# Attention features and a two-layer feed-forward: weights converted from one load by a rounded copy and a difference, with a new order of the first units

## The chip, the core and the metric

The kernel runs on one core of a Trainium2 chip. The metric is device time in microseconds, the median of three runs. The core's engines each work through their own queue in the order in which the program was written: TensorE (PE; its weight loads are PEld), VectorE (DVE), ScalarE (ACT), GpSimd (POOL) and SyncE (SP), which here issues nearly all DMAs.

## The reference

Eight batches of eight heads with 576 positions of 64 dimensions go through an attention with random features (128 features, each used with both signs), and the result, 4608 tokens of 512, through two matrix products with x·tanh(softplus(x)) between them.

```python
def phi(x):
    proj = np.einsum('bhsd,df->bhsf', x, w_phi)
    proj = proj - np.max(np.abs(proj), axis=-1, keepdims=True)
    return np.concatenate([np.exp(proj), np.exp(-proj)], axis=-1)
q_p, k_p = (phi(q), phi(k))
kv = np.einsum('bhsf,bhsd->bhfd', k_p, v)
z = np.sum(k_p, axis=2)
num = np.einsum('bhsf,bhfd->bhsd', q_p, kv)
den = np.einsum('bhsf,bhf->bhs', q_p, z)[..., None] + 1e-06
out = num / den
...
h = x @ w_in                     # 512 -> 2048
g = h * np.tanh(log1p(exp(h)))   # h itself where h > 20
return (g @ w_out).astype(np.float32)
```

w_in and w_out come as 64-bit floats; q, k, v and w_phi as 32-bit floats.

## The kernel before

**Work units.** Keys come in 36 units of 512 rows ("k0" to "k35"), queries in 18 chunks of 256 tokens with two halves each ("q0_0", "q0_1", "q1_0", ...), the values v in 32 tiles. A key unit is loaded, projected on TensorE (`project`, into two tiles pp), its absolute maximum is taken and subtracted on VectorE (`centre`: two reductions, two subtractions), ScalarE takes both exponentials (`exp`), and TensorE adds the products with v (`sum`, into kvps). A query unit is projected and centred likewise, turned, and multiplied with the finished sums (`num`), divided on VectorE (`divide`), turned again (`out q0_0`), and split into a high and a low half (`high` on ScalarE, `low` on VectorE).

**Feed-forward.** For chunk c, `in c f` multiplies the tokens with 128 columns of w_in (12 matmuls of 256 columns: high by high, low by high, high by low, over four pieces of 128 rows). ScalarE takes the nonlinearity (`mish`), and `out c f` multiplies with 128 rows of w_out (six matmuls of 512 columns in the first chunks). From chunk 4 on a form with fewer products is used for the second matrix.

**Weight pieces.** w_in has 16 pieces ("in", i, j) of 128x512 and w_out has 16 pieces ("out", i, 0). Each arrives as pairs of 32-bit words of its 64-bit numbers (`load_weight`, tile words_in or words_out). ScalarE copies the upper word's magnitude (`magnitude`, step "abs"). VectorE then bounds it (`split_clamp`), shifts it into the place of a 32-bit float (`split_shift`), and sets sign and top exponent bit (`split_sign`). The mask 0x3FFFF000 leaves a short mantissa, so the high part is exact in the matmul's format, and ScalarE writes it (`high_weight`, step "ready"). The low part is made apart. For 29 of the 32 pieces a second DMA (`load_middle`) brings the same numbers shifted by 16 bits, VectorE shifts these (`split_rest`), takes the power of two of the high part (`split_power`), and multiplies both (`split_low`, step "split"). The last three pieces build the rest from the two words in scratch instead.

**What sets the order.** `Plan.order` sorts tasks by keys (FIRST_KEYS, FIRST_QUERIES, WKEYS for the weights, step times for later units), lets each engine take the first task whose inputs are due by assumed durations, and so writes each engine's queue once for all. After that, before the change, it reorders the first 11 loads (NLOADS; those of v are put VLATE = 4.5 places later) and moves four loads of weights behind the load of v5 (LATER). All loads are issued by SyncE in this order. In the chip's run the queues have no freedom left: an instruction whose input is late holds up all that stand behind it on its engine. Loads of more than the first eight units share buffers, so a load can wait for a `project`.

**Names in the prediction.** The first chunk's products with the first four pieces of w_in are "in 0 0" to "in 0 3"; "out 0 3" is its product with the fourth piece of w_out. In the trace lines, `in` is L575, `out` of the first chunks L610, `sum` and `num` L401, `project` L360, a low half of a weight L307, the copies of a high half L326.

Of the kernel before, what the change touches and what calls it, by code (L numbers as in the profile page):

```python
# [17 lines left out]
P = 128  # L18
# [32 lines left out]
EARLY = 2.042  # L51
RAMP = (5, 3)
SOONER = 1.5
# [4 lines left out]
FIRST_KEYS = {0: -15.83, 1: -13.11, 2: -9.97, 3: -9.13, 4: -7.79, 5: 5.39, 6: 7.33, 7: 10.36, 8: 12.26, 9: 26.17, 10: 26.27}  # L58
FIRST_QUERIES = {0: -11.55, 1: -8.5, 2: -1.4, 3: -0.74, 4: 12.74, 5: 12.11}
# [7 lines left out]
E0 = 0.138  # L67
E1 = 0.171
GX = 0.403
ET = 0.107  # L70
WKEYS = [-6.42, -8.84, -5.8, -0.77, 4.55, 2.54, 6.13, 9.34, 4.27, 5.56, 11.66, 11.19, 18.21, 21.9, 23.26, 22.05,
         25.09, 22.07, 26.7, 34.84, 24.54, 37.47, 32.85, 40.81, 37.93, 41.3, 40.78, 41.2, 43.66, 37.64, 39.51, 45.36]
LAG, TAIL, TAILLAG = 4, 10, 2
TWOH = 10
HFIRST = 0.0
# [4 lines left out]
TLEAD = 3.609  # L80
SPLITC = 12
QFIRST = 99
URGENT = 2.061
UCENTRE = -0.136
# [4 lines left out]
class Plan:  # L89
# [11 lines left out]
    def order(self):  # L101
# [86 lines left out]
        at = [n for n, task in enumerate(tasks) if task["name"].startswith("load ")][:NLOADS]  # L188
        loads = sorted(range(NLOADS), key=lambda i: i + VLATE * tasks[at[i]]["name"].startswith("load v"))
        for n, task in zip(at, [tasks[at[i]] for i in loads]):  # L190
            tasks[n] = task
        moved = [next(task for task in tasks if task["name"] == name) for name in LATER]
        tasks = [task for task in tasks if task["name"] not in LATER]
        at = 1 + next(n for n, task in enumerate(tasks) if task["name"] == LATER_THAN)
        return tasks[:at] + moved + tasks[at:]
# [3 lines left out]
def attention_then_mish(ctx, tc, qT, kT, va, w_phi, w_in, w_out, out):  # L199
# [24 lines left out]
    weight, finished, homes_of, to_add, middles, rests = {}, {}, {}, {}, {}, {}  # L224
# [4 lines left out]
    def slot_tile(slot, dtype, name, words=None):  # L229
        return const.tile([P, words] if words else [P, 2, 512], dtype, tag=slot, name=name)  # L230
# [11 lines left out]
    def octets(kind, i, j):  # L242
        return w_in[i * P:(i + 1) * P, j * 512:(j + 1) * 512] if kind == "in" else w_out[i * P:(i + 1) * P, :]
# [23 lines left out]
    def parts_of(piece):  # L267
        words = weight[piece].rearrange("p (a b) -> p a b", b=2)
        if piece in middles:
            return words, middles[piece].bitcast(U32).rearrange("p (a b) -> p a b", b=2)  # L270
        if piece not in rests:
            nm = "%s_%d_%d" % piece
            rests[piece] = (scratch(f"rest_{nm}", f"rest:{piece}", U32),
                            work.tile([P, 512], U32, tag="half", name=f"t_{nm}", bufs=NHALF))
        return words, None

# [4 lines left out]
    def split_rest(piece):  # L281
        words, middle = parts_of(piece)
        if middle is not None:
            nc.vector.tensor_scalar(middle[:, :, 0], middle[:, :, 0], 7, None, op0=ALU.logical_shift_left)
        else:
            rest = rests[piece][0]
            nc.vector.tensor_scalar(rest, words[:, :, 1], 23, None, op0=ALU.logical_shift_left)
            nc.vector.scalar_tensor_tensor(rest, words[:, :, 0], 9, rest, op0=ALU.logical_shift_right, op1=ALU.bitwise_or)
# [5 lines left out]
    def split_sign(piece):  # L294
        w = to_add[piece]
        words = weight[piece].rearrange("p (a b) -> p a b", b=2)
        nc.vector.scalar_tensor_tensor(w, words[:, :, 1], 0xC0000000, w, op0=ALU.bitwise_and, op1=ALU.bitwise_or)

    def split_power(piece):
        words, middle = parts_of(piece)  # L300
        t = rests[piece][1] if middle is None else middle[:, :, 1]
        nc.vector.tensor_scalar(t, to_add[piece], 0xFF800000, None, op0=ALU.bitwise_and)

    def split_low(piece):
        _, middle = parts_of(piece)
        rest, t = rests[piece] if middle is None else (middle[:, :, 0], middle[:, :, 1])
        nc.vector.scalar_tensor_tensor(both(piece)[1], like(piece, rest), 2.0 ** -43, like(piece, t.bitcast(F32)),  # L307
                                       op0=ALU.mult, op1=ALU.mult)
# [15 lines left out]
    def high_weight(kind, i, j):  # L324
        piece = kind, i, j
        nc.scalar.copy(both(piece)[0], like(piece, to_add.pop(piece).bitcast(F32)))  # L326
# [532 lines left out]
    for t, is_query, n in units:  # L859
# [5 lines left out]
        if not is_query:  # L865
# [12 lines left out]
            for k, (p, parts) in enumerate(mine):  # L878
# [17 lines left out]
                if steady:  # L896
                    sums_at.setdefault(n - LEAD, []).append(f"sum {unit} {p}")
                add(f"sum {unit} {p}", "PE", sums, 0.05 + 0.466 * len(parts), lambda n=n, p=p, last=last: k_sum(n, p, last),
                    deps=deps, after=[f"sum {unit} {mine[k - 1][0]}"] if k else [],
# [54 lines left out]
    nmiddle = len(pieces) - len(homes)  # L954
    for i, pc in enumerate(pieces):
        nm, slot = f"{pc}", slots[i]
        ahead = [f"split {pieces[i - NAHEAD]}"] if i >= NAHEAD else []
        used = [f"split {pieces[n]}" for n in range(nmiddle) if homes[n % len(homes)] == slot]
        add(f"load {nm}", "SP", -47.5 + i * 0.1, 0.42, lambda pc=pc: load_weight(*pc),
            deps=last_use.get(slot, []) + used, after=ahead, take=[(slot, f"w:{nm}")], size=524288)  # L960
        if i < nmiddle:
            home = homes[i % len(homes)]
            add(f"middle {nm}", "SP", -47.45 + i * 0.1, 0.42, lambda pc=pc, home=home: load_middle(*pc, home),
                deps=last_use.get(home, []), take=[(home, f"m:{nm}")], size=524288)
# [4 lines left out]
        own = i >= nmiddle  # L969
        split("clamp", 0.34, split_clamp, [f"abs {nm}"])  # L970
        split("rest", 0.95 if own else 0.34, split_rest, [f"load {nm}" if own else f"middle {nm}"],
              take=[("part", f"rest:{nm}"), ("half", f"t:{nm}")] if own else [])
# [4 lines left out]
        add(f"ready {nm}", "ACT", WKEYS[i] + 0.1, 0.55, lambda pc=pc: high_weight(*pc), deps=[f"sign {nm}", f"power {nm}"], give=[f"u:{nm}", f"w:{nm}"])  # L977

# [150 lines left out]
    with tc.manual_schedule(engines={mybir.EngineType.PE, mybir.EngineType.DVE, mybir.EngineType.Activation, mybir.EngineType.SP}):  # L1129
        trial = bank("att", [P, P], "trial")  # L1130
        for _ in range(NTRIAL):
            nc.tensor.matmul(trial, ident, ident, start=True, stop=True)
        for task in plan.order():
            task["fn"]()

# [32 lines left out]
```

## Time and profile before

| | |
|---|---|
| three runs | 1046.14, 1047.18, 1042.16 us |
| median of them | 1046.14 us |
| profiled execution, span from first to last instruction | 1043.5 us |
| PE busy | 1029.5 us, 99% |
| DVE busy | 738.0 us, 71% |
| ACT busy | 655.6 us, 63% |
| moved by DMA | 223.09 MB, mean 214 GB/s |
| mean granted TensorE clock | 0.998 of full speed |

The profiled execution's own device time is not listed apart from its span. The span lies between the lowest and the middle of the three runs. A share of busy time is a mean over the whole execution. Stages differ: in the first 100 us attention units and all the weight conversion fall together, later an even step repeats. TensorE's matmuls overlap one another, so their busy time says only where the engine had nothing at all to do. The times of single instructions on VectorE and ScalarE overlap by about 0.09 us with the next one's start, so a price per instruction is read from start to start.

### The profile page before, as it was taken

How to read it: one execution, taken by the hardware profiler on the slowest of the kernel's cores; microseconds unless marked ns; L12 is line 12 of the kernel's file. 1: busy time of each engine (PE TensorE's matmuls, PEld its weight loads, DVE VectorE, ACT ScalarE, POOL GpSimd, SP SyncE). 2: the span in 40 equal slices, each digit the busy share in tenths (PEclk: the TensorE clock that was granted, in tenths of full speed). 3: DMA queues.
4: the chain of work that ended last, by engine and by line, in shares of the span. 5: the costliest groups of instructions: out<-in, count | busy, mean ns of one | idle time of the engine just before them, and what ended most of it. 6: DMA issues, size and time to landing. Idle time of an engine off the chain costs nothing.

```text
span 1043.5 us, 30075 instructions
## 1 busy us (share of the span) xinstructions
PE 1029.5 (99%) x12286; PEld 990.6 (95%) x12286; DVE 738.0 (71%) x1692; ACT 655.6 (63%) x1028; POOL 0.7 (0%) x6
## 2 busy tenths in 40 slices
PE   8999999999999999999999999999999999999998
PEld 7888998899889999999999999999999999999998
DVE  7998998677886675767676767675776666666553
ACT  6799898667665756666666656665665565545532
POOL 0000000000000000000000000000000000000000
PEclk9999999999999999999999999999999999999999
DMA  9768664465977666767667564757576666765844
GB/s 319 271 235 317 189 209 136 125 204 160 296 246 235 212 211 205 222 215 226 216 209 230 193 209 159 242 186 243 175 237 196 206 189 212 219 220 190 291 142 155
DMA packets 158313, 223.09 MB, mean 214 GB/s; under 512 B 17120, under 2 KB 75616, under 8 KB 158176
## 3 DMA queue, kind: packets, MB, share of 16 engines
q1 hardware_dynamic: 158032, 221.11, 64.8%
q8 instruction: 97, 1.59, 0.6%
q14 instruction: 40, 0.33, 0.1%
q10 hardware_dynamic: 144, 0.07, 0.0%
HBM read 177.59 MB, written 43.52 MB: 212 GB/s over the span
## 4 chain that ended last, share of the span: by engine, by line
PE 93%; DVE 3%; DMA 3%; issue 1%; SPq 1%; ACT 0%; DVEq 0%; ACTq 0%
PE h L575 38%; PE oy L745 8%; PE ox L745 8%; PE o L610 8%; PE ow L745 8%; PE num L401 7%; PE kvps L401 6%; PE oz L745 4%; PE pp_q L360 4%; PE pp_k L360 3%; DMA middle_in<-w_in 1%; DMA words_out<-w_out 1%; DMA v<-va 1%; DMA words_in<-w_in 0%; PE dt L480 0%
## 5 line engine op out<-in xcount | busy, mean ns | idle before, releaser
L575 PE MATMUL h<-xTh,win 128*128 128x256 f32 x2304 | 429.1, 280 | 1.0 <-DVE e_k L372 1.0
L575 PEld LDWEIGHTS h<-xTh,win 128*128 128x128 f32 x2304 | 361.0, 188 | 5.2 <-PE h L575 1.2
L575 PE MATMUL h<-xTl,win 128*128 128x256 f32 x1152 | 321.9, 279 | 0.0
L575 PEld LDWEIGHTS h<-xTl,win 128*128 128x128 f32 x1152 | 216.5, 188 | 1.8
L660 DVE TENSOR_TENSOR sl<-s,sh 128x640 fp32r<-128x640 f32 x112 | 92.0, 823 | 106.7 <-ACT sh L656 101.7
L656 ACT CAST sh<-s 128x640 fp32r<-128x640 f32 x112 | 80.7, 722 | 90.8 <-DVE s L651 79.2
L641 ACT ACTIVATE u<-h 128x512 f32<-128x512 f32 x112 | 66.9, 598 | 96.2 <-PE h L575 95.7
L649 DVE TENSOR_TENSOR s<-u 128x256 f32<-128x256 f32 x112 | 46.9, 418 | 90.5 <-ACT u L641 90.3
L401 PEld LDWEIGHTS kvps<-v,e_k 128*64 128x64 f32 x2560 | 78.4, 137 | 9.4 <-issue 4.2
L401 PE MATMUL kvps<-v,e_k 128*64 128x66 f32 x2560 | 84.0, 223 | 3.2 <-issue 2.5
L745 PE MATMUL oy<-wout,sh 128*128 128x256 f32 x448 | 85.7, 284 | 0.0
L745 PE MATMUL ox<-wout,gh 128*128 128x256 f32 x440 | 83.6, 283 | 0.0
L745 PE MATMUL ow<-wout,sh 128*128 128x256 f32 x440 | 82.9, 281 | 0.0
L610 PE MATMUL o<-wout,gh 128*128 128x512 f32 x256 | 81.7, 400 | 0.0
L401 PE MATMUL num<-kv,e_q 128*64 128x66 f32 x2304 | 78.1, 225 | 1.8 <-DVE xTl L559 1.0
L401 PEld LDWEIGHTS num<-kv,e_q 128*64 128x64 f32 x2304 | 73.2, 139 | 4.9 <-issue 1.5
L436 ACT ACT_TABLE_LOAD x25 | 32.1, 1283 | 64.9 <-DVE e_k L372 64.5
L745 PEld LDWEIGHTS oy<-wout,sh 128*128 128x128 f32 x448 | 68.5, 188 | 1.6
L745 PEld LDWEIGHTS ox<-wout,gh 128*128 128x128 f32 x440 | 67.2, 188 | 0.7
L745 PEld LDWEIGHTS ow<-wout,sh 128*128 128x128 f32 x440 | 67.4, 188 | 0.0
L745 PE MATMUL oy<-wout,sl 128*128 128x256 f32 x224 | 62.9, 281 | 0.0
L745 PE MATMUL ow<-wout,sl 128*128 128x256 f32 x220 | 61.7, 280 | 0.0
(120 smaller groups left out, 1824.4 us busy)
## 6 DMA issues: line engine op xcount, KB each, us to landing
wout<-terms SPq DMA_DIRECT2D x344, 256.0 KB, 4.6
there_e<-e_q SPq DMA_DIRECT2D x60, 256.0 KB, 2.6
e_q<-there_e SPq DMA_DIRECT2D x240, 64.0 KB, 2.3
v<-va SPq DMA_DIRECT2D x32, 330.0 KB, 4.8
out<-osb SPq DMA_DIRECT2D x35, 256.0 KB, 2.6
raw_k<-kT SPq DMA_DIRECT2D x34, 256.0 KB, 3.5
raw_q<-qT SPq DMA_DIRECT2D x34, 256.0 KB, 3.5
there_x<-via SPq DMA_DIRECT2D x30, 256.0 KB, 2.0
```

The costliest lines, as they stand in the source:

```text
L360: nc.tensor.matmul(ps[j][:, n], raw[rows, n * P:(n + 1) * P], w_phi2[rows], start=True, stop=True)
L401: nc.tensor.matmul(ps[rows], lhsT[h], rhs[h], start=start, stop=stop, skip_group_check=True)
L436: nc.scalar.activation(e[:, 1, :], e[:, 0, :], AF.Exp)
L575: nc.tensor.matmul(ps, w[:, wcol], x[:, cc % 2, :], start=(n == 0), stop=(n == 11))
L610: nc.tensor.matmul(ps.rearrange("p (k n) -> p k n", k=2), g[:, cols], w, start=(i == first and k == 0), stop=(i == end and k == 2))
L641: nc.scalar.activation(u, h_live.pop((c, fp)).rearrange("p f s -> p (f s)"), AF.Mish)
L649: nc.vector.tensor_tensor(s[:, :CH], u[:, :CH], u[:, CH:], op=ALU.add)
L656: nc.scalar.copy(mix_high[c, fp], mixed[c, fp])
L660: nc.vector.tensor_sub(mix_low[c, fp], mixed.pop((c, fp)), mix_high[c, fp].bitcast(F32))
L745: nc.tensor.matmul(ps, a, b, start=(begins and n == 0 and (apart or not half)), stop=(ends and n == 2), skip_group_check=True)
```

## The change

Weights: `load_middle`, `split_rest`, `split_power` and the tiles for them are gone. The shifted magnitude keeps all its bits (mask 0x3FFFFFF8), a new step `split_tail` puts three bits of the lower word behind it, and so a whole 32-bit float of the weight stands in w. ScalarE's `high_weight` rounds it into the matmul's format, and `split_low` subtracts that rounded copy from w on VectorE.

Order: new numbers in all tables of keys; the rearrangement of the first 11 loads and of LATER is gone; a `sum` of one v tile is now held behind the sum of the unit before it. At the end of TensorE's queue twelve matmuls are added that write a tile nobody reads.

```diff
-EARLY = 2.042
+EARLY = 2.102
-FIRST_KEYS = {0: -15.83, 1: -13.11, 2: -9.97, 3: -9.13, 4: -7.79, 5: 5.39, ...
+FIRST_KEYS = {0: -33.11, 1: -30.69, 2: -9.44, 3: -8.85, 4: -7.78, 5: -6.87, ...
-NLOADS = 11
-LATER = ["load ('in', 0, 1)", "load ('out', 0, 0)", "load ('out', 2, 0)", "load ('out', 3, 0)"]
-LATER_THAN = "load v5"
-VLATE = 4.5
...
-        at = [n for n, task in enumerate(tasks) if task["name"].startswith("load ")][:NLOADS]
-        loads = sorted(range(NLOADS), key=lambda i: i + VLATE * tasks[at[i]]["name"].startswith("load v"))
...
-        return tasks[:at] + moved + tasks[at:]
+        return tasks
...
-    def load_middle(kind, i, j, home):
-        middle = middles[kind, i, j] = slot_tile(home, U16, f"middle_{kind}_{i}_{j}", 2048)
-        in_parts(middle[:, :2046], octets(kind, i, j).bitcast(U16)[:, 1:2047])
...
     def split_shift(piece):
         w = to_add[piece]
-        nc.vector.tensor_scalar(w, w, 3, 0x3FFFF000, op0=ALU.logical_shift_left, op1=ALU.bitwise_and)
+        nc.vector.tensor_scalar(w, w, 3, 0x3FFFFFF8, op0=ALU.logical_shift_left, op1=ALU.bitwise_and)
+
+    def split_or(piece, half, scalar, op):
+        w = to_add[piece]
+        words = weight[piece].rearrange("p (a b) -> p a b", b=2)
+        nc.vector.scalar_tensor_tensor(w, words[:, :, half], scalar, w, op0=op, op1=ALU.bitwise_or)
...
+    def split_tail(piece):
+        split_or(piece, 0, 29, ALU.logical_shift_right)
...
     def split_low(piece):
-        nc.vector.scalar_tensor_tensor(both(piece)[1], like(piece, rest), 2.0 ** -43, like(piece, t.bitcast(F32)),
-                                       op0=ALU.mult, op1=ALU.mult)
+        hi, lo = both(piece)
+        nc.vector.tensor_sub(lo, like(piece, to_add.pop(piece).bitcast(F32)), hi.bitcast(F32))
...
-        split("power", 0.34, split_power, [f"sign {nm}", f"rest {nm}" if own else f"middle {nm}"])
-        split("split", 0.61, split_low, [f"power {nm}", f"rest {nm}"], give=[f"rest:{nm}", f"t:{nm}"] if own else [f"m:{nm}"])
-        add(f"ready {nm}", "ACT", WKEYS[i] + 0.1, 0.55, ..., deps=[f"sign {nm}", f"power {nm}"], ...)
+        split("tail", 0.61, split_tail, [f"sign {nm}"])
+        add(f"ready {nm}", "ACT", WKEYS[i] + 0.1, 0.55, ..., deps=[f"tail {nm}"])
+        split("split", 0.61, split_low, [f"ready {nm}"], give=[f"u:{nm}", f"w:{nm}"])
...
+        for _ in range(3):
+            nc.tensor.matmul(last, hi[:, :P], hi, start=True, stop=True)
+        for _ in range(4):
+            nc.tensor.matmul(last[:, :256], hi[:, :P], hi.rearrange("p (a b) -> p a b", a=2)[:, :, :P], start=True, stop=True)
+        for _ in range(5):
+            nc.tensor.matmul(last[:, :P], hi[:, :P], hi[:, P:2 * P], start=True, stop=True)
```

Where the order is new, three places show it. The first is the head of SyncE's queue, the loads at the start of the program; raw_k0 is one buffer that takes key unit 0 (in four parts) and then key unit 1, raw_q0_0 one for the first queries and key unit 2. Before:

```order
L352 DMA raw_k0_89<-kT 128x128 x4
L352 DMA raw_k0_89<-kT 128x512
L352 DMA raw_q0_0_95<-qT 128x512
L352 DMA raw_q0_0_95<-kT 128x512
L431 DMA v_0_98<-va 128x660
L352 DMA raw_k3_100<-kT 128x512
L431 DMA v_1_102<-va 128x660
L352 DMA raw_k3_100<-qT 128x512
```

and now:

```order
L317 DMA raw_k0_89<-kT 128x128 x4
L396 DMA v_0_94<-va 128x660
L317 DMA raw_k0_89<-kT 128x512
L396 DMA v_1_97<-va 128x660
L317 DMA raw_q0_0_99<-qT 128x512
L317 DMA raw_q0_0_99<-kT 128x512
L396 DMA v_2_102<-va 128x660
L317 DMA raw_k3_104<-kT 128x512
```

The loads of v0 and v1 have moved ahead of key unit 1 and of the first queries.

The second place is VectorE's queue at some 24 us, the conversion of the first pieces of w_in; words and w belong to a weight piece, win is its finished half, r and x to a division of queries, m and e to a centring. Before:

```order
L302 TENSOR_SCALAR middle_in_0_0_126<-w_in_0_0_276 128x512
L297 SCALAR_TENSOR_TENSOR w_in_1_0_371<-words_in_1_0_137,w_in_1_0_371 128x512
L523 TENSOR_SCALAR r1_0_0_473<-num1_0_0_438 128x4
L524 RECIPROCAL r1_0_0_473<-r1_0_0_473 128x4
L525 TENSOR_TENSOR x_0_0_415<-num1_0_0_438,r1_0_0_473 128x256
L302 TENSOR_SCALAR middle_in_1_0_150<-w_in_1_0_371 128x512
L307 SCALAR_TENSOR_TENSOR win_0_0_485<-middle_in_0_0_126 128x512
L307 SCALAR_TENSOR_TENSOR win_1_0_487<-middle_in_1_0_150 128x512
L364 TENSOR_REDUCE m0_k4_511<-pp0_k4_463 128x4
L364 TENSOR_REDUCE m1_k4_513<-pp1_k4_464 128x4
L372 TENSOR_TENSOR e0_k4_515<-pp0_k4_463,m0_k4_511 128x512
L372 TENSOR_TENSOR e1_k4_517<-pp1_k4_464,m1_k4_513 128x512
```

and now:

```order
L263 SCALAR_TENSOR_TENSOR w_in_1_0_341<-words_in_1_0_126,w_in_1_0_341 128x512
L263 SCALAR_TENSOR_TENSOR w_in_3_0_373<-words_in_3_0_150,w_in_3_0_373 128x512
L436 COPY kv_1_460<-kvps_1_279 128x264
L263 SCALAR_TENSOR_TENSOR w_in_3_0_373<-words_in_3_0_150,w_in_3_0_373 128x512
L273 TENSOR_TENSOR win_1_0_458<-w_in_1_0_341,win_1_0_458 128x512
L329 TENSOR_REDUCE m0_k4_502<-pp0_k4_447 128x4
L329 TENSOR_REDUCE m1_k4_504<-pp1_k4_448 128x4
L337 TENSOR_TENSOR e0_k4_506<-pp0_k4_447,m0_k4_502 128x512
L337 TENSOR_TENSOR e1_k4_508<-pp1_k4_448,m1_k4_504 128x512
L488 TENSOR_SCALAR r1_0_0_553<-num1_0_0_485 128x4
L489 RECIPROCAL r1_0_0_553<-r1_0_0_553 128x4
L490 TENSOR_TENSOR x_0_0_393<-num1_0_0_485,r1_0_0_553 128x256
```

The low half (L307 before, L273 now) stands behind three or more other instructions, and the division of num1_0_0 has moved behind the centring of key unit 4.

The third place is the end of TensorE's queue, where ow1_17 is the last product of the last chunk. Now:

```order
L710 MATMUL ow1_17_14892<-late_0_14319,sh_17_1_15102 128x256 x2
L710 MATMUL ow1_17_14892<-late_0_14319,sl_17_1_15118 128x256
L710 MATMUL ow1_17_14892<-late_2_14618,sh_17_0_15172 128x256 x2
L710 MATMUL ow1_17_14892<-late_2_14618,sl_17_0_15174 128x256
L1094 MATMUL last_15233<-win_0_0_679 128x512 x3
L1096 MATMUL last_15233<-win_0_0_679 128x256 x4
L1098 MATMUL last_15233<-win_0_0_679 128x128 x5
```

The rows of `last` are new, the branch behind them is the end of the program.

## Rows read from the trace of the kernel before

**Rows 1.** Windows of all engines: us, busy (instructions) by engine, PEclk, DMA share, GB/s.
```profile
0.00:20.00 20.00, 17.14 (x270) 15.70 (x272) 13.18 (x25) 10.68 (x18) 0.70 (x6) 1.00 0.90 310
20.00:40.70 20.70, 16.87 (x400) 15.18 (x396) 19.05 (x46) 16.82 (x41) 0.00 (x0) 1.00 0.85 293
40.70:44.10 3.40, 3.40 (x60) 3.34 (x62) 3.37 (x8) 1.79 (x4) 0.00 (x0) 0.50 1.02 397
44.10:86.00 41.90, 40.11 (x516) 35.84 (x513) 39.50 (x92) 37.72 (x61) 0.00 (x0) 1.00 0.74 255
86.00:1040.00 954.00, 951.89 (x11057) 920.57 (x11055) 662.47 (x1524) 588.59 (x907) 0.00 (x0) 1.00 0.64 208
```

**Rows 2.** Windows cut where VectorE's first work and the place stand.
```profile
5.17:44.00 38.83, 33.58 (x698) 30.98 (x700) 35.52 (x76) 28.01 (x60) 0.00 (x0) 0.96 0.93 332
44.00:74.00 30.00, 28.42 (x409) 26.53 (x406) 28.51 (x69) 26.39 (x42) 0.00 (x0) 1.00 0.66 221
```

**Rows 3.** Timeline, TensorE and VectorE: start, us, engine, line, out<-in [idle <-releaser].
```profile
73.13 0.69 PE L401 MATMUL kvps<-v,e_k 128*64 128x66 f32 x16 [0.66 <-DMA v<-va]
73.75 0.73 PE L610 MATMUL o<-wout,gh 128*128 128x512 f32 x2
...
73.34 0.69 DVE L307 SCALAR_TENSOR_TENSOR wout<-middle_out 128x512 fp32r<-128x512 uint32 x1
```

**Rows 4.** Timeline of VectorE, two maxima and a centring.
```profile
10.21 1.28 DVE L364 TENSOR_REDUCE m_q<-pp_q 128x4 f32<-128x512 f32 x2
...
12.61 1.28 DVE L364 TENSOR_REDUCE m_k<-pp_k 128x4 f32<-128x512 f32 x2
```

**Rows 5.** Timeline of VectorE in the conversion of two pieces.
```profile
23.81 0.42 DVE L292 TENSOR_SCALAR w_in<-w_in 128x512 uint32<-128x512 uint32 x1
24.15 0.42 DVE L302 TENSOR_SCALAR middle_in<-w_in 128x512 uint32<-128x512 uint32 x1
...
27.30 1.29 DVE L307 SCALAR_TENSOR_TENSOR win<-middle_in 128x512 fp32r<-128x512 uint32 x2
```

**Rows 6.** Groups to 200 us: form, count, busy us, mean ns, idle before.
```profile
L693 DVE TENSOR_TENSOR comb<-comb,combh 128x512 fp32r<-128x512 f32 x2 | 1.4, 693 | 0.1
...
L581 ACT ACT_TABLE_LOAD x16 | 20.5, 1283 | 0.3
...
L326 ACT CAST win<-w_in 128x512 fp32r<-128x512 f32 x16 | 9.9, 626 | 1.4 <-DVE w_in L297 1.4
```

**Rows 7.** Timeline of VectorE, three of its waits.
```profile
18.27 0.43 DVE L284 TENSOR_SCALAR middle_in<-middle_in 128x512 uint32<-128x512 uint32 x1 [1.46 <-DMA middle_in<-w_in]
...
26.22 0.16 DVE L523 TENSOR_SCALAR r<-num 128x4 f32<-128x4 f32 x1 [1.05 <-PE num L401]
...
54.16 0.69 DVE L559 TENSOR_TENSOR xTl<-xt,xTh 128x512 fp32r<-128x512 f32 x1 [0.61 <-ACT xTh L553]
```

**Rows 8.** Chain of waits at the start; DMA issues (KB each, us to landing).
```profile
2.59 3.07 DMA raw_k<-kT
...
v<-va SPq DMA_DIRECT2D x32, 330.0 KB, 4.8
```

**Rows 9.** Chain of waits, groups of matmuls in two stretches.
```profile
101.42 1.87 PE kvps L401 x64
...
127.66 2.02 PE kvps L401 x64
129.68 1.60 PE h L575 x12
...
132.69 1.40 PE h L575 x12
```

**Rows 10.** Timeline of TensorE, its last matmul.
```profile
1039.82 0.28 PE L745 MATMUL ow<-late,sl 128*128 128x256 f32 x1
```

**Rows 11.** Waits of TensorE after 200 us: total, times, longest.
```profile
PE h L575 <- DVE e_k L372: 1.0, 1, 1.0
```

**Rows 12.** Timeline of ScalarE, key unit 3's exponentials.
```profile
21.23 4.23 ACT L386 ACTIVATE e_k<-pp_k,mm_k 128x128 f32<-128x128 f32 x16
```

More of the change, by code (lines that the diff above doesn't have):

```diff
@@ L50 @@
 NTHERE = 8
-EARLY = 2.042
+EARLY = 2.102
 RAMP = (5, 3)
-SOONER = 1.5
+SOONER = 1.447
 SOONER_STEPS = (9, 14)
@@ L223, in attention_then_mish @@
     pieces += [("out", 12 + i, 0) for i in range(4)]
-    weight, finished, homes_of, to_add, middles, rests = {}, {}, {}, {}, {}, {}
+    weight, finished, homes_of, to_add = {}, {}, {}, {}
     slots = [f"w{kind}_{i}_{j}" for kind, i, j in pieces]
@@ L265, in magnitude @@
         nc.scalar.activation(w.bitcast(F32), high.bitcast(F32), AF.Abs)
[L267 to L275, printed above, removed]
     def split_clamp(piece):
@@ L325, in high_weight @@
         piece = kind, i, j
-        nc.scalar.copy(both(piece)[0], like(piece, to_add.pop(piece).bitcast(F32)))
+        nc.scalar.copy(both(piece)[0], like(piece, to_add[piece].bitcast(F32)))
     raws, shared, projected, maxima, features = {}, {}, {}, {}, {}
@@ L898, in attention_then_mish @@
                 add(f"sum {unit} {p}", "PE", sums, 0.05 + 0.466 * len(parts), lambda n=n, p=p, last=last: k_sum(n, p, last),
-                    deps=deps, after=[f"sum {unit} {mine[k - 1][0]}"] if k else [],
+                    deps=deps, after=([f"sum {unit} {mine[k - 1][0]}"] if k else []) + ([] if begins else [f"sum k{n - 1} {p}"]),
                     near=[f"exp q{(n - LEAD) // 2}_{(n - LEAD) % 2} {j}" for j in range(2)] if steady and n >= LEAD + 2 * NTURNED else [], take=take, give=give)
@@ L957, in attention_then_mish @@
         ahead = [f"split {pieces[i - NAHEAD]}"] if i >= NAHEAD else []
-        used = [f"split {pieces[n]}" for n in range(nmiddle) if homes[n % len(homes)] == slot]
         add(f"load {nm}", "SP", -47.5 + i * 0.1, 0.42, lambda pc=pc: load_weight(*pc),
[L960 to L964, printed above, removed]
+            deps=last_use.get(slot, []), after=ahead, take=[(slot, f"w:{nm}")], size=524288)
         add(f"abs {nm}", "ACT", WKEYS[i] - 0.5, 0.55, lambda pc=pc: magnitude(*pc), deps=[f"load {nm}"], take=[("w", f"u:{nm}"), ("part", f"w:{nm}")])
@@ L967, in split @@
             add(f"{step} {nm}", "DVE", WKEYS[i], took, lambda pc=pc, fn=fn: fn(pc), deps=deps, late=0.13, **more)
-        own = i >= nmiddle
         split("clamp", 0.34, split_clamp, [f"abs {nm}"])
-        split("rest", 0.95 if own else 0.34, split_rest, [f"load {nm}" if own else f"middle {nm}"],
-              take=[("part", f"rest:{nm}"), ("half", f"t:{nm}")] if own else [])
         split("shift", 0.34, split_shift, [f"clamp {nm}"])
         split("sign", 0.61, split_sign, [f"shift {nm}"])
-        split("power", 0.34, split_power, [f"sign {nm}", f"rest {nm}" if own else f"middle {nm}"])
-        split("split", 0.61, split_low, [f"power {nm}", f"rest {nm}"], give=[f"rest:{nm}", f"t:{nm}"] if own else [f"m:{nm}"])
-        add(f"ready {nm}", "ACT", WKEYS[i] + 0.1, 0.55, lambda pc=pc: high_weight(*pc), deps=[f"sign {nm}", f"power {nm}"], give=[f"u:{nm}", f"w:{nm}"])
+        split("tail", 0.61, split_tail, [f"sign {nm}"])
+        add(f"ready {nm}", "ACT", WKEYS[i] + 0.1, 0.55, lambda pc=pc: high_weight(*pc), deps=[f"tail {nm}"])
+        split("split", 0.61, split_low, [f"ready {nm}"], give=[f"u:{nm}", f"w:{nm}"])
     tiles = [(c, f) for part in range(2) for c in range(2) for f in range(4 * part, 4 * part + 4)]
@@ L1134, in attention_then_mish @@
             task["fn"]()
+        hi = finished["in", 0, 0][0]
+        last = bank("h", [P, 512], "last")
+        for _ in range(3):
[4 more added lines that the diff above has]
+            nc.tensor.matmul(last[:, :P], hi[:, :P], hi[:, P:2 * P], start=True, stop=True)
 def kernel(q, k, v, w_phi, moe_w_in, moe_w_out):
```

48 lines of the change are left out of this document (14 added, 34 removed).

## Prediction

> **What bounds the kernel now.** I read the windows first, engine by engine [rows 1]. From 86 us on TensorE is busy for all but 2.1 us of 954, so there are two microseconds to win in that part. In the first 86 us it is idle 2.86 + 3.83 + 1.79 us, and for 3.4 us its clock stands at 0.50, the lower of its two levels. What can be gained or lost lies there. In the same stretch VectorE is nearly full: 35.52 of 38.83 us and 28.51 of 30.00 us [rows 2], so it waits 3.31 + 1.49 = 4.80 us in all between its first instruction and 74 us.
>
> The place that sets the end is the product "out 0 3". At 73.75 us TensorE begins it, 0.4 us after VectorE began the low half of its weight piece, the fourth of w_out [rows 3]; the low half is read from the second matmul on. Just ahead TensorE waited 0.66 us for a v; had that come sooner, it would have waited for the low half instead. Behind it TensorE has nearly nothing to wait for, so every microsecond by which this place moves is a microsecond at the end. I counted VectorE's instructions up to that low half in both orders and priced them from start to start: a centring is 2.40 us (12.61 − 10.21) [rows 4]; an operation with one tensor 0.33 us (24.15 − 23.81) and one with two tensors 0.60 us (two of them end after 1.29, the last of which is 0.69 long) [rows 5]. The windows give 35.52 + 28.51 = 64.0 us of VectorE work [rows 2]: 11 centrings are 26.4 of them, the conversion of ten pieces 24.6 (below), and 13.0 are left for key unit 3's maxima, 8 divisions, 2 copies and 7 low halves of activations. From 5.17 us on, with 4.80 us of waits, that is 74.0 us, where the low half ends (73.34 + 0.69). So the place is a VectorE sum plus its waits.
>
> **The change, part by part.**
>
> *Conversion.* Before, a piece with a second load takes four one-tensor operations and two two-tensor ones: 4 × 0.33 + 2 × 0.60 = 2.52 us. Now it takes clamp, shift, sign, tail and a subtraction: 2 × 0.33 + 3 × 0.60 = 2.46. The subtraction is priced by a row of its form, 128x512 to fp32r, at 693 ns [rows 6], as long as the other two-tensor operations. Up to the place the old order has done ten pieces but for one low half (40 × 0.33 + 19 × 0.60 = 24.6), the new one ten whole pieces (20 × 0.33 + 30 × 0.60 = 24.6). Everything else up to there has the same count. The gain in VectorE work is 0.0 us here; the three pieces that had no second load save 0.66 us each, far behind the place, where TensorE does not wait.
>
> *Second loads.* 29 loads of 0.52 MB, 15.2 MB, are gone. Their price is in waits only: the wait of 1.46 us for the first middle at 18.27 us [rows 7] goes, −1.46 us (between −1.46 and 0, if the word load is late in its place). Later waits for such loads lie behind the place and cost nothing now.
>
> *Order of the first loads.* v0 now stands ahead of key unit 1, and v1 ahead of the first queries. In the trace unit 1 lands 3.07 us after its issue at 2.59, and VectorE's second centring starts on it without slack. A v is 330 KB [rows 8], 338 kB, at the 310 GB/s of the first 20 us 1.09 us. +1.1 us (0 if the transfers overtake, 2.2 if the queries' unit comes late by both). The Trainium skill ("DMA: Bandwidth & Descriptors", "Queues, rings and completion order") says that a DMA engine takes descriptors in ring order though completions are not in order; this speaks for the full 1.1. No run so far shows the pair in this order.
>
> *Order of the first units.* Before, VectorE waits 1.05 us at 26.22 for the numerator of the first queries [rows 7], with one division as the next thing in its queue. Now the centring of key unit 4 (2.40 us) stands ahead of that division, while the numerator has moved behind a transposition, a projection and part of a sum, about 2 us of TensorE. I take −1.05 (between −1.05 and +1.05).
>
> *A longer chain.* Before, the low half needed nothing from ScalarE. Now it is the difference to the rounded copy, so VectorE waits for a ScalarE cast of 0.62 us [rows 6], and what is queued behind it is the next centring or division, on which TensorE's next group hangs. In the new order at least two whole operations, 1.2 us of VectorE work, stand between tail and difference of each of the ten pieces (the fewest at w_out's first piece), which covers a cast if ScalarE is free. VectorE's waits for ScalarE's activation casts, 0.61 us the longest [rows 7], show what one such miss costs. I take one, +0.6 us (0 to 10 × 0.62 = 6.2).
>
> *TensorE's groups.* A feed-forward group of 12 takes 1.60 us behind a group of half-height matmuls and 1.40 elsewhere; 64 matmuls of a sum take 2.02 us behind feed-forward work and 1.87 elsewhere [rows 9]. Such changes of kind number 111 before and 117 now, 19 of them ahead of the place in both. Six more at (0.20 + 0.15) / 2 is +1.0 us (0 to 1.0).
>
> *The twelve matmuls at the end.* They begin behind the last product, which starts at 1039.82 [rows 10]. A feed-forward matmul of 256 columns is issued every 0.117 us (1.40 / 12) [rows 9], so three of 512 columns and nine of 256 or fewer take at most 3 × 0.233 + 9 × 0.117 = 1.75 us and end by 1042. The last sums and stores cover them up to the span's end at 1043.5: 0 us, and at most 1 without that cover, if leaving TensorE takes as long as leaving the stores does.
>
> *Tables of ScalarE.* The order has 152 loads of a table against 136, 16 more of 1.28 us [rows 6]. They stand in the steady part; from 86 us on ScalarE is idle for over a third of the time [rows 1], which hides 20.5 us: nothing (0 to 1, the size of the one wait for a key unit there [rows 11]).
>
> Sum: −1.46 + 1.1 − 1.05 + 0.6 + 1.0 = +0.2 us on the span of 1043.5, so 1043.7. The profiled execution's span lies 2.6 us under the median of the three runs and 1.7 us under their mean (1045.2). I add the 1.7: **1045.4 us, no change**. Runs of this kernel spread by 5 us, 0.5%, and I take less than that (1040.9 to 1051.4) as no change.
>
> **The rivals.**
>
> *VectorE runs without waits (faster).* If the shorter load queue and the new order take every wait, the place comes 4.80 us earlier, v0 and v1 ahead cost nothing, and the one longer wait of the steady part, 1.0 us [rows 11], goes too: −5.8 + 1.0 for the changes of kind, and no more than 0.3 for the rest, 1045.2 − 5.1 = 1040.1. For it: a third of the waits are on the second loads, and two TensorE stalls in mid group without a releaser stand where the DMA share is 0.85 to 0.90 [rows 1]. Against it: the waits on TensorE and ScalarE are a matter of order and are only exchanged. Chance 0.20.
>
> *The difference waits for the cast (slower).* ScalarE is busy 26.39 of 30.00 us from 44 to 74 [rows 2], with six table loads in the new order's stretch. If each cast stands behind one other instruction, all ten differences wait about a cast: +6.2 us, with the changes of kind 1045.2 + 7.2 = 1052.4. It decides from about nine of ten on (5.2 us). Against it: the 1.2 us of cover or more. Chance 0.17.
>
> *The wait moves to the word loads.* The third piece that is converted is now ("in", 3, 0), with 7 units, 5 v and 4 pieces loaded up to it: 5.62 MB. At the 310 GB/s of the first 20 us [rows 1] it is there at 18.1 us, at the 250 GB/s by which the first middle came (4.57 MB by 18.27) at 22.5. ScalarE takes its magnitude ahead of key unit 3's exponentials, which began at 21.23 [rows 12]; with 0.6 us for the magnitude they would slip 1.9 us. The change then doesn't free the loads as it says: 1045.4 + 1.9 = 1047.3. Chance 0.13.
>
> *The clock falls in the feed-forward work.* From 40.70 to 44.10 the clock was at 0.50, after a stretch in which TensorE was busy 16.87 of 20.70 us [rows 1]; half of 3.4 us of matmul time was lost, in front of a wait for VectorE, so almost nothing. Now the largest waits stand around "in 1 0" and "out 0 3", where a fall meets TensorE's own work. Two falls: 1045.4 + 3.4 = 1048.8. The Trainium skill ("TensorE: Matmul & The Clock Gate", "HAM oscillation — how this bites in real kernels") warns of just this, bursts between waits that each start at the low clock; the trace has it once within the work. Chance 0.10.
>
> **How the numbers follow.** Forecast 0.40, the four rivals 0.20, 0.17, 0.13 and 0.10. Within 0.5% lie the forecast and the last two: 0.63. Faster 0.20, slower 0.17. The range goes from 1039.5, just under the fast rival, to 1051.0, short of the slow one: some 0.08 is left out below and 0.12 above. The forecast's own terms at their ends, without the long chain, give −2.5 to +4.3 us around 1045.2.
>
> **What would show it.** In the new profile "out 0 3" starts between 73 and 75 us; no VectorE wait for a middle; the second centring starts near 8.9 instead of 7.81; one or two short VectorE waits on the cast; TensorE idle after 86 us 2 to 3 us. I am wrong if "out 0 3" starts before 71 or after 77 us, if the differences wait for the cast more than three times before 74 us, or if TensorE's idle time after 86 us passes 5 us.

## The result, and the profile after

The changed kernel takes 1055.65 us, the median of four runs (1054.80 to 1056.23); the kernel before 1044.21, the median of four runs, three of them the ones listed ahead. The ratio is 1.0107, with a 95% interval of 1.0084 to 1.0131: slower by 11 us, 1.1%, where 1045.4 and no change were predicted, and outside the range of 1039.5 to 1051.0. The profiled execution of the changed kernel took 1056.23 us, with a span of 1054.4.

The windows of the new profile, cut as in [rows 1]:
```profile
0.00:20.00 20.00, 17.37 (x254) 15.82 (x254) 12.60 (x23) 10.18 (x17) 0.70 (x6) 1.00 0.89 315
20.00:40.70 20.70, 18.55 (x455) 16.79 (x454) 19.24 (x43) 16.93 (x42) 0.00 (x0) 1.00 0.46 168
40.70:44.10 3.40, 3.35 (x60) 2.83 (x62) 3.40 (x8) 2.22 (x5) 0.00 (x0) 1.00 0.82 254
44.10:86.00 41.90, 39.04 (x483) 34.78 (x484) 39.23 (x84) 37.18 (x60) 0.00 (x0) 0.96 0.51 162
86.00:1040.00 954.00, 947.01 (x10956) 912.68 (x10955) 655.22 (x1490) 609.33 (x919) 0.00 (x0) 1.00 0.62 198
```
Up to 86 us TensorE's busy time has changed little, 78.3 us against 77.5. Behind it TensorE is idle for 954.00 − 947.01 = 6.99 us, where it was 2.1: the mark of 5 us that the prediction set for being wrong is passed.

The place the prediction argued about came out as forecast by its number. TensorE's and VectorE's timelines of the changed kernel, to set beside [rows 3]:
```profile
72.45 2.09 PE L366 MATMUL kvps<-v,e_k 128*64 128x66 f32 x64
74.47 0.73 PE L575 MATMUL o<-wout,gh 128*128 128x512 f32 x2
...
74.06 0.68 DVE L273 TENSOR_TENSOR wout<-w_out,wout 128x512 fp32r<-128x512 f32 x1
```
"out 0 3" starts at 74.47, in the forecast 73 to 75, again 0.4 us behind its low half. But here VectorE doesn't set it. The sum ahead of it runs into it without a wait, VectorE's own last wait, 0.40 us at 71.66, is for TensorE, and TensorE's last long wait ahead of all this is for ScalarE's high half of the tokens, xTh. ScalarE writes it at 59.23, behind a mish and a magnitude that each load a table (54.69 to 58.58):
```profile
59.86 0.38 PE L540 MATMUL h<-xTh,win 128*128 128x256 f32 x1 [2.19 <-ACT xTh L518]
```
From there to "out 0 3" TensorE has no other wait over 0.34 us, and the granted clock stood at 0.57 from 60 to 64 us.

Most of the loss stands in two stretches that the prediction never opened. The same windows, cut finer, first of the kernel before:
```profile
86.00:140.00 54.00, 54.00 (x614) 49.17 (x613) 48.42 (x116) 48.96 (x89) 0.00 (x0) 1.00 0.70 235
140.00:160.00 20.00, 20.00 (x203) 18.12 (x203) 18.34 (x45) 18.21 (x27) 0.00 (x0) 1.00 0.54 176
...
345.00:1030.00 685.00, 684.32 (x8160) 674.59 (x8159) 451.31 (x1055) 397.30 (x596) 0.00 (x0) 1.00 0.65 211
```
and of the changed one:
```profile
86.00:140.00 54.00, 54.00 (x534) 49.14 (x533) 43.32 (x98) 46.54 (x82) 0.00 (x0) 1.00 0.35 130
140.00:160.00 20.00, 16.42 (x132) 13.94 (x132) 19.12 (x39) 18.19 (x28) 0.00 (x0) 0.98 0.18 54
160.00:170.00 10.00, 10.00 (x174) 8.94 (x172) 8.17 (x16) 9.50 (x15) 0.00 (x0) 0.87 0.13 35
...
345.00:1030.00 685.00, 683.25 (x8122) 671.53 (x8122) 449.39 (x1051) 422.25 (x614) 0.00 (x0) 1.00 0.66 209
```
Two things are to be seen. From 140 to 160 us TensorE is idle 3.58 us where it was not idle at all, and the granted clock falls to 0.87 in the ten microseconds behind. And from 345 to 1030 us TensorE does 38 matmuls fewer than before in the same time; at 685 / 8160 = 0.084 us each that is about 3 us, of which the profile shows 1.07 us more as idle time. ScalarE is busy 25 us longer there.

The first of the two in TensorE's timeline: two waits, 2.77 of the 3.58 us, are for key unit 9's exponentials (0.60 us more is for a rounded copy of a weight, 0.22 for a difference), and the 56 matmuls behind them take 3.35 us.
```profile
158.22 0.45 PE L366 MATMUL kvps<-v,e_k 128*64 128x66 f32 x8 [2.04 <-ACT e_k L402]
159.40 3.35 PE L366 MATMUL kvps<-v,e_k 128*64 128x66 f32 x56 [0.73 <-ACT e_k L402]
```
That these exponentials fall here is the work of the new order. Key unit 9's projection, before:
```profile
103.22 1.16 PE L360 MATMUL pp_k<-w_phi,raw_k 64*128 64x128 f32 x16
```
and now:
```profile
146.58 1.16 PE L325 MATMUL pp_k<-w_phi,raw_k 64*128 64x128 f32 x16
```
What ScalarE did meanwhile, in its own timeline of the changed kernel:
```profile
147.09 0.60 ACT L546 ACTIVATE u<-h 128x512 f32<-128x512 f32 x1
147.71 0.71 ACT L549 CAST gh<-u 128x256 fp32r<-128x256 f32 x2
148.45 1.28 ACT L250 ACT_TABLE_LOAD   x1
149.74 0.68 ACT L250 ACTIVATE w_out<-words_out 128x512 f32<-128x512 f32 x1
150.32 0.60 ACT L291 CAST win<-w_in 128x512 fp32r<-128x512 f32 x1
150.83 0.66 ACT L250 ACTIVATE w_out<-words_out 128x512 f32<-128x512 f32 x1
152.29 0.62 ACT L291 CAST wout<-w_out 128x512 fp32r<-128x512 f32 x1 [0.79 <-DVE w_out L263]
152.93 1.28 ACT L546 ACT_TABLE_LOAD   x1
...
155.59 1.28 ACT L401 ACT_TABLE_LOAD   x1
156.88 0.63 ACT L401 ACTIVATE e_k<-e_k 128x512 f32<-128x512 f32 x1
```
A weight piece passes ScalarE twice, for its magnitude (L250) and for its rounded copy (L291). It did so before; new is that its low half waits for the second pass too. Where a magnitude stands behind a mish, it loads a table of 1.28 us, and so does the next mish. The planner counts 0.55 us for a magnitude and no table.

In what follows "lag" is the start of one of TensorE's groups less the work of all groups ahead of it at fixed prices (1.03 us for a projection, 1.40 for a feed-forward group of 12, 0.175 for a change of kind, and so on), summed over the matmuls of the trace. It rises where TensorE loses time. Between 345 us and the end it grows by 3.5 us before and by 7.8 after. The lag is a reckoning and no view of the profile, but it can be checked without any prices. The projection of key unit 18, before:
```profile
356.65 1.16 PE L360 MATMUL pp_k<-w_phi,raw_k 64*128 64x128 f32 x16
```
and after:
```profile
363.09 1.16 PE L325 MATMUL pp_k<-w_phi,raw_k 64*128 64x128 f32 x16
```
From there up to the last product stand the same 8045 matmuls, and that product starts 683.2 us later before (at 1039.82) and 687.6 us later after (at 1050.70). So of the 10.9 us by which the last product is late, 0.7 arise ahead of "out 0 3", 5.7 between it and key unit 18, and 4.4 behind.

### The profile page after: what moved, and what is told of

It reads as the page before. It is cut to its first block, busy times and chain, and to the rows that moved or that the text cites. A ratio compares the mean times of both kernels' runs of the same rounds, so it can differ in the third digit from the quotient of the medians.

```text
span 1054.4 us, 30049 instructions
## 1 busy us (share of the span) xinstructions
PE 1038.0 (98%) x12298; PEld 995.3 (94%) x12298; DVE 734.7 (70%) x1657; ACT 678.2 (64%) x1044; POOL 0.7 (0%) x6
## 4 chain that ended last, share of the span: by engine, by line
PE 88%; ACT 6%; DVE 3%; issue 1%; DMA 1%; SPq 0%; ACTq 0%; DVEq 0%
PE h L540 35%; PE oy L710 7%; PE ox L710 7%; PE o L575 7%; PE ow L710 7%; PE kvps L366 7%; PE num L366 6%; PE pp_q L325 4%; PE oz L710 4%; PE pp_k L325 3%; DMA wout<-terms 1%; ACT L546 1%; ACT L250 0%; ACT sh L621 0%; DVE sl L625 0%
```

## The experiments

All twelve were timed beside the kernel before on one chip each time (before: 1043.9 to 1045.0 in the median). Four theories were in play: that the order loses the time, that the conversion loses it in any order, and, from the seventh run on, that ScalarE (C) or VectorE (D) is late in 86 to 190 us.

**1. The conversion alone.** New conversion; keys, constants and moved loads as before.
```
-FIRST_KEYS = {0: -33.11, ..., 9: 27.26, 10: 28.81}
+FIRST_KEYS = {0: -15.83, ..., 9: 26.17, 10: 26.27}
-E0 = -0.966
+E0 = 0.138
...
```


> The kernel before with the new conversion alone: no shifted second loads, the difference behind ScalarE's cast, but the keys of the first units and of the pieces, the constants of the steady part and the moved loads as before, without the twelve matmuls at the end. From key unit 13 on the order on TensorE, VectorE and ScalarE is that of before. Theory (the loss sits in the order of units, not in the conversion): within 3 us of before, 1041 to 1047 us. Rival 1 (differences wait for the casts): 1050 us or more, with VectorE waits for ScalarE's weight casts of 5 us in all or more. Rival 2 (fewer loads free the start): 1041 us or less.

1057.17 us, ratio 1.0121 (1.0106 to 1.0136). The time is not the theory's but lies in the range of rival 1. It is as slow as the whole change, but not by the same loss: from 345 to 1030 us TensorE does 8158 matmuls, about as many as before (8160), so all of it arises earlier. The waits in 86 to 345 us, of TensorE and of VectorE (total, times, longest):
```profile
PE h L551 <- DVE win L284: 4.9, 1, 4.9
...
DVE wout L284 <- ACT wout L302: 7.0, 2, 5.3
```
A difference stood behind its cast for 5.3 us, and TensorE waited 4.9 us for a low half. But the order up to key unit 13 was one that the planner made anew, so conversion and order were still mixed.

**2. Key units 9 and 10 earlier.**
```
-FIRST_KEYS = {... 9: 27.26, 10: 28.81}
+FIRST_KEYS = {... 9: 20.0, 10: 22.0}
```


> The changed kernel with two numbers of its table of first keys changed: key unit 9 from 27.26 to 20.0 and key unit 10 from 28.81 to 22.0, so that TensorE projects them behind 'in 2 3' and 'out 2 1' instead of behind 'in 2 11' and 'out 2 8'. Theory (the wait of 'sum k9 8' and the half clock behind it cost 5.3 us, and nothing takes their place): 1050 us, TensorE's lag no longer jumps between 146 and 190 us. Rival 1 (the lag only hides another wait that comes next, VectorE being as full as before): 1054 to 1056 us. Rival 2 (all of the loss is in the steady part): 1055 us.

1053.66 us, 1.0087 (1.0074 to 1.0101). The wait at 158 us went (20.00 of 20.00 us busy from 140 to 160), but 2.0 of the 5.3 us came back as time; 1.41 us of TensorE's idle time stand in the next stretch:
```profile
170.00:190.00 20.00, 18.59 (x205) 15.30 (x206) 13.80 (x29) 13.37 (x22) 0.00 (x0) 1.00 0.47 148
```
Mostly rival 1: another wait takes the place.

**3. The steady part's constants set back.**
```
-E0 = -0.966
+E0 = 0.138
-HFIRST = 0.226
+HFIRST = 0.0
...
```


> The changed kernel with the ten constants of the steady part set back (EARLY, SOONER, E0, E1, GX, ET, HFIRST, TLEAD, URGENT, UCENTRE). From key unit 13 on the order on TensorE, VectorE and ScalarE is that of before, up to there that of the changed kernel; ScalarE loads 16 tables fewer. Theory (some 4 us are lost bit by bit in the steady part's own order, 0.4 us in two changes of kind): 1051 us, the jump at 146 to 190 us as in the changed kernel. Rival 1 (the steady part loses only because it begins late and cold): 1055 us. Rival 2 (the conversion or the twelve matmuls lose it): 1055 us.

1052.70 us, 1.0079 (1.0065 to 1.0093), 3 us less than the changed kernel. The lag from 345 us on grows by 3.7 us, as before, and the matmuls are back:
```profile
345.00:1030.00 685.00, 684.36 (x8160) 674.65 (x8159) 451.46 (x1056) 400.75 (x600) 0.00 (x0) 1.00 0.65 210
```

**4. Both edits.**
```
+FIRST_KEYS = {... 9: 20.0, 10: 22.0}
+E0 = 0.138
...
```


> The changed kernel with both edits: key units 9 and 10 at 20.0 and 22.0, and the ten constants of the steady part set back. TensorE changes kind 121 times instead of 117. Theory (the two losses add up): 1055.7 - 5.3 - 4.4 + 0.7 = 1046.7 us, 1045 to 1049. Rival 1 (conversion and loads lose most): 1052 us or more. Rival 2 (the two are one loss, the late start of the steady part): the same as the better of the two alone, about 1050 us.

1054.90 us, 1.0095 (1.0080 to 1.0110): a miss, 2.2 us above the third run in the median. TensorE's waits in 190 to 345 us show a new one, of 3.3 us:
```profile
PE h L540 <- ACT u L606: 3.3, 1, 3.3
```
Two orders that each gain make a third that loses somewhere else. Here, what an order costs could not be added up from edits of keys.

**5. The new conversion in the old order.** So the order was pinned: the names of before's tasks in before's sequence.
```
     def order(self):
+        names, self.place = json.loads(zlib.decompress(base64.b85decode(PINNED)))
+        return [self.named[name] for name in names]
```


> The new conversion in the order of the kernel before, written out as a list of names instead of planned: TensorE, ScalarE and SyncE do what they did before in the same order (SyncE without the 29 shifted loads), VectorE too, but that the operation with the low word stands where the power's mask stood, the operations on the shifted halves are gone, and 13 of 32 differences stand one to five operations later, behind the place where the cast is planned to end. Theory A (the conversion costs nothing by itself; the first run of this study lost 12 us because the planner made an order of its own that nobody had fitted): 1041 to 1047 us, TensorE idle 2 us at most after 86 us. Theory B (the cast in the middle of the chain costs it in any order): 1049 us or more, with VectorE waiting 5 us or more for ScalarE's weight casts and TensorE for win or wout.

1047.60 us, 1.0026 (1.0016 to 1.0036): between the theories. The conversion by itself costs 2.7 us (1.7 to 3.8) in an order that was fitted to the other one. So some 10 of the first run's 12.6 us came with the order that the planner made there (1.0121 against 1.0026). VectorE's waits for ScalarE on weights, in 74 to 200 us:
```profile
DVE wout L405 <- ACT wout L423: 2.7, 5, 1.0
...
DVE w_in L386 <- ACT w_in L382: 1.5, 2, 0.9
DVE win L405 <- ACT win L423: 1.5, 2, 1.1
```

**6. The new constants in the old kernel**, the mirror of the third.
```
-E0 = 0.138
+E0 = -0.966
-HFIRST = 0.0
+HFIRST = 0.226
...
```


> The kernel before, with its conversion, its loads and its keys, and the ten constants of the steady part (EARLY, SOONER, E0, E1, GX, ET, HFIRST, TLEAD, URGENT, UCENTRE) taken from the changed kernel. Up to 'project k9' TensorE's order is that of before but for one exchange of a numerator and a transposition. Theory (these constants cost 4 us between 345 us and the end, in gaps too short to be listed as waits, and 0.4 us for changes of kind): TensorE's lag grows by 7 to 8 us from 345 us to the end instead of 3.5, and the time is 1045 + 4.3 = 1049 us, if the order up to 345 us stays as good as before, 1048 to 1053 in all. Rival (the gaps come with the new conversion or with a late start): the lag grows by 3.5 to 4 us there, the time is within 1.5 us of before.

1050.50 us, 1.0055 (1.0040 to 1.0069). The lag from 345 us on grows by 7.9 us, with the old conversion and an early start, so neither of these makes the loss of the steady part. From key unit 18 on it takes 686.4 us, 3.2 more than before; about as much again of the loss arises ahead of that.
```profile
345.00:1030.00 685.00, 683.01 (x8123) 671.54 (x8122) 450.38 (x1053) 421.81 (x612) 0.00 (x0) 1.00 0.65 209
```

**7. The changed kernel without ScalarE's magnitudes.**
```
-        nc.scalar.activation(w.bitcast(F32), high.bitcast(F32), AF.Abs)
...
-        nc.vector.tensor_scalar(wf, wf, LARGE, SMALL, op0=ALU.min, op1=ALU.max)
+        nc.vector.tensor_scalar(wf, high.bitcast(F32), LARGE, -LARGE, op0=ALU.min, op1=ALU.max)
```


> The changed kernel in its own order, without ScalarE's 32 magnitudes of weight pieces (0.67 us each, and the table loads that they cause behind a mish): VectorE's clamp reads the high words itself and clamps them with their sign. It leaves out the lower bound of the magnitude, which no weight but zero or below 2^-127 meets. VectorE has as many operations as before. Theory C (from 86 to 190 us ScalarE is what makes the differences and the exponentials of key unit 9 late, since every piece now passes through it twice before it is done): the wait of 'sum k9 8' and the half clock behind it go, 1055.5 - 5 = 1050.5 us, and VectorE's waits for ScalarE in 74 to 200 us fall from some 7 us to under 3. Theory D (VectorE's own queue is what is late there): 1054 to 1056 us.

1048.82 us, 1.0043 (1.0030 to 1.0057): 6.7 us less than the changed kernel by the ratios, with the same order on every engine. Theory C. "project k9" stands where it stood in that order, and the wait behind it is gone:
```profile
86.00:140.00 54.00, 54.00 (x532) 49.10 (x531) 47.08 (x105) 33.17 (x68) 0.00 (x0) 1.00 0.32 117
140.00:160.00 20.00, 20.00 (x251) 17.54 (x252) 19.07 (x38) 13.47 (x23) 0.00 (x0) 1.00 0.16 54
```
ScalarE is busy 33.17 us of the 54 instead of 46.54, and VectorE, which waits less, does 105 operations there instead of 98. VectorE's waits for ScalarE in 74 to 200 us fell from 7.8 us to 5.1, less far than expected; those on weights fell from 5.6 to 1.0, the rest are for the feed-forward work. ScalarE had cost time ahead of 74 us too: the wait for xTh is 0.38 us here, with 0.77 for its low half, and "out 0 3" starts at 72.70.

**8. The same in the old order** (the fifth run without magnitudes).


> The kernel of the fifth run (new conversion in the old order), again without ScalarE's magnitudes, the clamp reading the high words itself and leaving out the lower bound that no weight here meets. Theory C: VectorE's 5.1 us of waits for weight casts fall to 2 us or less, and the 2.7 us that the conversion cost in this order go: 1045 us or less. Theory D: within 1 us of the fifth run, 1047 us.

1045.03 us, 1.0008 (0.9999 to 1.0017): by the ratios 1.9 of the 2.7 us of the conversion go, and the interval does not tell the other 0.8 from nothing. Over the first 200 us the waits for casts went only from 5.1 to 4.5 us (none over 0.7); what went are the 2.6 us of waits for magnitudes. So the time came as theory C says, the waits not quite.

**9. The same in the kernel before.**


> The kernel before, its conversion and order unchanged, without ScalarE's magnitudes in the same way. Theory C: before, a piece's low half did not need ScalarE after the magnitude and TensorE waits for little behind 86 us, so at most the 2 us of waits for magnitudes go: 1043 to 1045 us. If it is 1040 us or less, ScalarE bounded the start already before the change.

1044.57 us, 1.0004 (0.9995 to 1.0014). ScalarE had much the same load before, and it cost nothing that shows: a piece's low half hung on the magnitude, but not on the cast behind it.

**10. HFIRST alone in the kernel before.**
```
-HFIRST = 0.0
+HFIRST = 0.226
```


> The kernel before with one constant of the changed one, HFIRST 0.226 instead of 0 (the half of a unit whose product stands in the feed-forward bank is taken first on VectorE). ScalarE's planned changes of table rise from 124 to 136, TensorE's changes of kind from 111 to 115. Theory (of the ten constants this one makes the loss of the steady part, by the order of the exponentials): TensorE's lag grows by 7 to 8 us from 345 us to the end instead of 3.5, 1049 to 1050 us. Rival (the loss needs several of them): the lag grows by less than 5 us, 1045 to 1047 us.

1050.45 us, 1.0062 (1.0050 to 1.0074). Of the ten constants this one makes the loss by itself; by matmuls done it is even a little more than all ten:
```profile
345.00:1030.00 685.00, 682.15 (x8102) 669.71 (x8101) 449.01 (x1049) 411.64 (x603) 0.00 (x0) 1.00 0.64 208
```
The lag was not worked out here. From key unit 18's projection (355.22) to the last product (1044.55) it takes 689.3 us, 6.2 more than before. ScalarE is busy 14 us longer than before from 345 to 1030 us. Whether its table loads do it or the order of the exponentials was not told apart.

**11. Both causes taken away** (the third and the seventh together).


> The changed kernel with the ten constants of the steady part set back (as in the third run) and without ScalarE's magnitudes (as in the seventh; the lower bound that no weight here meets is left out). Theory (the constants and ScalarE's place in the chain are the whole loss, and they add up): 1052.7 - 6.7 = 1046 us by the third run, 1048.8 - 4.2 = 1044.6 by the seventh, so 1044 to 1047; TensorE idle under 3 us after 86 us. Rival (the two overlap, since both load ScalarE): 1048 us or more. Rival (something of the new order of the first units is still lost): 1048 us or more, with a wait of TensorE behind 86 us that names it.

1045.73 us, 1.0008 (0.9999 to 1.0017). The two add up, and what is left of the 11 us is 0.8, which the interval does not tell from nothing. From 140 to 160 us TensorE is busy throughout, and the steady part is as before:
```profile
345.00:1030.00 685.00, 684.33 (x8156) 674.36 (x8155) 451.04 (x1055) 397.04 (x595) 0.00 (x0) 1.00 0.65 210
```

**12. No clamp either** (the eighth, with the shift reading the high words).
```
-        nc.vector.tensor_scalar(w, w, 3, 0x3FFFFFF8, op0=ALU.logical_shift_left, op1=ALU.bitwise_and)
+        nc.vector.tensor_scalar(w, high, 3, 0x3FFFFFF8, op0=ALU.logical_shift_left, op1=ALU.bitwise_and)
```


> The kernel of the eighth run (new conversion in the old order, no magnitude on ScalarE) without the clamp too: the shift reads the high words itself. It leaves out both bounds of the magnitude, which no weight here meets (they lie at 2^-127 and 2^128). VectorE has 32 operations of 0.33 us fewer, ten of them ahead of the product 'out 0 3'. Theory (up to 'out 0 3' the time is a VectorE sum plus its waits, as the prediction has it): that product starts 3.3 us earlier, near 69 instead of 72.2 us, and the time is 1045 - 3.3 = 1041.7 us, 1041 to 1043, under both kernels. Rival (something else is late there next, a load or TensorE's own chain): the product starts at 71 us or later and the time is 1044 us or more.

1042.76 us, 0.9980 (0.9967 to 0.9993): under both kernels, for weights between the two bounds. Its mechanism is not shown. The profiled execution, with 1045.87 us the longest of the eleven, has "out 0 3" at 72.60 (72.22 in the eighth run), with a wait of TensorE that is not there in the other, 0.89 us for a load of queries at 69.49. By that one trace the rival holds; by the ratios, 0.9980 against 1.0008, 2.9 of the expected 3.3 us came. That "out 0 3" is a VectorE sum stays open.

## Why the prediction was wrong

Two terms of the sum were mis-sized. In run 11, which takes away what stands behind both, 10.3 of the 11.2 us are gone (1.0107 against 1.0008).

*A longer chain, +0.6 (0 to 6.2): it measured 2.7 in the old order and, together with the new order, 6.7.* The prediction saw that the difference now hangs on ScalarE, and counted the ten pieces ahead of "out 0 3". There it was right: no difference waits for its cast before 74 us. But 22 of the 32 pieces are converted between 74 and 179 us, and for that part the prediction had one sentence, that ScalarE "is idle for over a third of the time" from 86 us on [rows 1]. It is, over 954 us. Before the change, from 86 to 140 it was busy 48.96 of 54.00 us, and from 140 to 160 18.21 of 20.00. In the old order that load was harmless with the old chain (run 9) and is harmless no longer when a piece must pass it once more before its last step: the conversion costs 2.7 us (run 5), of which 1.9 go with the magnitudes (run 8). In the changed kernel's order the same magnitudes cost 6.7 us (run 7; 7.4 between runs 3 and 11). How much of the 6.7 is the chain's and how much the order's is not shown, since no run has the old conversion in the new order; magnitudes alone were nothing new.

The trace has a part of both. VectorE's waits for ScalarE on weights, from 74 to 200 us, in the changed kernel:
```profile
DVE w_out L254 <- ACT w_out L250: 2.0, 2, 1.7
...
DVE w_in L254 <- ACT w_in L250: 1.5, 1, 1.5
DVE win L273 <- ACT win L291: 1.4, 1, 1.4
...
DVE wout L273 <- ACT wout L291: 0.7, 1, 0.7
```
and before:
```profile
DVE w_out L279 <- ACT w_out L265: 1.3, 2, 0.8
...
DVE w_in L279 <- ACT w_in L265: 0.8, 1, 0.8
```
The 2.1 us for casts (L291) are the chain's. The waits for magnitudes were there before, 2.1 us, and are 3.5 now; so it was not right that before "the low half needed nothing from ScalarE". The larger loss came as a second step: VectorE's conversions and ScalarE's tables made key unit 9's exponentials late, which the new order had put in this stretch. The rival "the difference waits for the cast" named the chain, but its condition, waits ahead of "out 0 3", did not come.

The Trainium skill ("ScalarE: Activation LUTs", "Table sets: the hidden batching unit") says that cheap functions such as abs "appear in *every* set as filler". By that a magnitude behind a mish would load nothing. The trace differs: seven table loads stand at L250 in the changed kernel, twelve at the same line before, 1.283 us each, and the measurement decides.

*TensorE's groups, +1.0, and tables of ScalarE, 0 (0 to 1): the steady part's constants measured 2.9 to 3.7* (1.0107 less 1.0079, and 1.0043 less 1.0008). The prediction priced ten constants by what can be counted in an order, changes of kind and tables. Behind key unit 18 TensorE lost 4.4 us more; the list of waits from 345 us on has 0.8 of them, and the profile shows 1.1 us more idle time than before in all; the rest passed while it counted TensorE as busy. One constant, HFIRST, suffices for such a loss; how it makes it is open.

*TensorE has nearly nothing to wait for behind "out 0 3"* was true of the old order and was carried over to a new one. Runs 1, 2 and 4 show how little that is justified: each had a wait of TensorE, of 4.9, 1.0 and 3.3 us, at a place of its own.

*The place is a VectorE sum plus its waits* held before and not in the changed kernel, where TensorE came to "out 0 3" from a wait for ScalarE at 59.86. So the 74.47 inside the forecast 73 to 75 is in part luck. Second loads, first loads, first units and the longer chain gave −1.46 + 1.1 − 1.05 + 0.6 = −0.8 there, and it starts 0.7 us later, 1.5 us off.

The other steps held. *Order of the first loads:* the second centring starts at 8.85, forecast 8.9:
```profile
8.85 1.29 DVE L329 TENSOR_REDUCE m_k<-pp_k 128x4 f32<-128x512 f32 x2 [0.82 <-PE pp_k L325]
```
*Second loads:* no wait for a middle is left, but its −1.46 was spent on other waits: from 5.17 to 74 us VectorE is idle 5.64 us, where it was 4.80. *The wait moves to the word loads* did not occur: ScalarE takes the third magnitude at 21.74 without waiting for its load. *The twelve matmuls:* the last product starts at 1050.70, the span ends at 1054.4, 3.7 us later as before [rows 10]; the twelve lie inside, from 1050.81 to 1052.65. *The clock falls in the feed-forward work:* it fell twice in the profiled execution, the number that this rival had named: behind the wait at 59.86 (0.57 from 60 to 64 us) and behind the one at 158 us (0.87 from 160 to 170). In runs 7 and 11, without the wait at 158 us, it stays at 1.00 there. But the falls are not the loss: of the changed kernel's four executions the one with a mean granted clock of 1.000 took 1055.36 us, and the one with the lowest, 0.995, took 1054.80, the least of the four.

## What to carry to other kernels

Ask of a new dependency how busy the engine is in every stretch in which it occurs: a share over the whole run hides the stretch in which that engine is full. To tell an edit's own cost from that of the order that a planner makes around it, pin the old order, and take the suspected engine's load away in the new one; what only the old edit in the new order could tell stays open without that run. Constants that only set an order can cost as much as an edit, mostly in time that no list of waits shows; count the work done in a fixed window. A forecast place that comes out is worth a look at what it waited for.

## What the runs showed of the hardware that was not expected

- A magnitude on ScalarE behind a mish loads a table of 1.283 us, and a mish behind a magnitude does too (148.45 and 152.93 us above). Behind an exponential it loads none: at 95.84 us in the changed kernel one follows an exponential begun at 94.87 directly. Without the 32 magnitudes ScalarE loads 140 tables instead of 152, and was busy 33.17 instead of 46.54 us from 86 to 140 us.
- The instruction behind a table load starts as it ends: 148.45 + 1.28 and 149.74.
- A one-tensor VectorE operation that reads every second word took as long here as one that reads adjacent ones: 16 clamps of w_out pieces take 417 ns each in run 7, where they read the high words, and 416 ns in the changed kernel.
